# Keys and values in tiles of 96 local and 32 global rows, and one bank that takes values and global scores before either is read

## The chip, the cores and the metric

The kernel runs on one core of a Trainium2 chip. Its metric is the device time of one execution in microseconds (us), the median of several runs; the kernel before took 952.92 us (952.77 to 953.38 in 3 runs). A core has engines that run side by side, each with its own in-order queue: TensorE (PE, matrix products, with weight loads as PEld), VectorE (DVE), ScalarE (ACT), GpSimd (POOL) and SyncE (SP), which here issues nearly all transfers (DMAs). TensorE writes its products to PSUM, which has eight banks of 128 partitions x 512 floats; DVE and ACT read them from there.

## The reference

Three stages follow each other. Attention over 4 batches, 8 heads, 512 local tokens and 32 global ones, with a head size of 64:

```
k_all, v_all = concat(k_g, k_l), concat(v_g, v_l)          # 32 + 512 rows
out_g = softmax(q_g k_all^T / 8) v_all                     # global queries see everything
s_ll  = q_l k_l^T / 8, only where |i - j| <= 32            # local queries see a band ...
out_l = softmax(concat(q_l k_g^T / 8, s_ll)) v_all         # ... and the 32 global keys
```

Its 2176 rows of 512 go through two MLPs with weights 512 x 2048 and 2048 x 512: first `h = x @ w_in; max(0.01 h, h) @ w_out`, then `h = x @ w_in; (h - tanh(h)) @ w_out`. The MLP weights arrive as 64-bit floats and are converted in the kernel; each product runs as three products of high and low parts.

## The kernel before, in words

Attention is cut into 32 units, numbered `pp`: a batch, a half `a` of its 512 queries (256 of them), and two of the eight heads. Four heads of a half make a group `g` (two units), which is what is loaded at once. The 256 queries of a unit are eight blocks of 32 (index `i`). A block sees three blocks of local keys and the 32 global ones, so its scores are 32 x 128: a window of 128 columns in the transposed keys.

- `load_kq(g)` (L331) loads queries `qr` and keys `kr`; `kr` holds 320 key rows in three tiles of 112, 112 and 96. `load_v(g)` (L356) loads values into one of three `v_raw` tiles, 96 local rows and, in the last 32 partitions, the global ones.
- `k_prep(pp)` (L393) transposes the keys on PE, then ACT (L402) and DVE (L404, L405) copy them to `kt`, with the global 32 columns repeated after each 96 local ones. `q_prep` does the same for the queries.
- `score(pp)` writes the windows of both heads to two banks; `smax_a` takes the row minimum (DVE, in the later units together with the mask, L457) and the exponential (ACT, L464).
- `p_trans(pp)` (L468) transposes the exponentials, and ACT copies them to `pt`.
- `copy_v(pp)` (L371) has POOL copy the values to `vx`, shifted, so that each window has its 128 value rows in the order of its columns; L378 first repeats the global rows.
- `av(pp, ps)` (L489) multiplies `pt` by the values into the columns 0 to 259 of the bank `avps` (64 value columns and a sum for each of four head and half combinations). DVE then reads the bank: L500 and L501 make the reciprocal of the sum, L503 the division into `o`. `o_trans` (L506) transposes `o` into the bank `otps`, and ACT and DVE make the MLP's inputs `xh` and `xl` of it.
- `g_score(pp, ps)` (L548) multiplies the keys by the global queries; ACT copies the result to `sg`. From unit 10 on (`PRE`) it writes the columns from 260 on of the same bank that `av` has just used; before that it has a bank of its own (`sgps`).

`stage(s)` (L864) puts units behind one another: in stage s the keys of unit s+1 are prepared, unit s is scored, `cols` (L870) does `av` of unit s-2 and `g_score` of unit s, and `turns` does `p_trans` of unit s-1 and `o_trans` of unit s-2. In `cols` the order is: `av` with its reads by DVE, then `load_v`, `copy_v`, then `g_score` with its read by ACT.

Stages 0 to 9 come first, with little else on PE. Stages 10 to 33 lie between the steps of the first MLP (`mlp1_a` makes `h`, `mlp1_b` makes `y`): their operations are spread over its items, one after every few groups of three matmuls. From unit 10 on the stages use three banks in turn. Weights are converted beside them (`in_job`, `job`: L127, L131, L137, L142, then L149/L150 or L785/L788).

The order of PE is the written one as far as attention reaches (`fix`, L940, switches the planner off for PE). The other engines, SP's transfers among them, are ordered by a planner that simulates the program; each of them then works in that order and stands when its next instruction has to wait.

Of the kernel before, what the change touches and what calls it, by code (L numbers as in the profile page):

```python
# [8 lines left out]
F32 = mybir.dt.float32  # L9
# [12 lines left out]
def kernel(  # L22
# [265 lines left out]
    band = att.tile([BLK, 3 * BLK], mybir.dt.bfloat16, name="band", bufs=1)  # L288
# [5 lines left out]
    def build_masks():  # L294


# [3 lines left out]
        for at, step in ((0, 1), (2 * BLK, -1)):  # L300
# [6 lines left out]
        for i in range(8):  # L307
            j, u = divmod(i, 4)
            n = BLK * (3 - i % 3)
            for a in range(2):  # L310
                m = mask[BLK * u : BLK * u + BLK, a, j]
                nc.vector.tensor_copy(m[:, :n], band[:, :n])
                if n < 3 * BLK:
                    nc.vector.tensor_copy(m[:, n + BLK :], band[:, n:])
        nc.vector.memset(mask[:BLK, 0, 0, :BLK], BIG)
        nc.vector.memset(mask[3 * BLK :, 1, 1, 3 * BLK :], BIG)

    first_key = [0, SL - 288]
    KT = (0, 112, 224, 320)

# [3 lines left out]
    v_raw = [att.tile([128, 4, 4, D + 1], F32, name=f"vr{i}", bufs=1) for i in range(3)]  # L324
# [6 lines left out]
    def load_kq(g):  # L331
# [4 lines left out]
        qr = att.tile([128, 2, 4, D], F32, tag="qr", name="qr", bufs=2)  # L336
        kr = att.tile([128, 3, 4, D], F32, tag="kr", name="kr", bufs=2)

        for t in range(3):
            on = nc.scalar if g == 0 and t == 2 else nc.sync  # L340
            for r0, r1, loc in ((0, SG, a), (SG, 9 * BLK, 1), (9 * BLK, 10 * BLK, not a)):
                lo, hi = max(r0, KT[t]), min(r1, KT[t + 1])
                if lo >= hi:
                    continue
                k0 = a * HALF - BLK + lo
                src = k_l[b, hs, k0 : k0 + hi - lo, :] if loc else k_g[b, hs]
                on.dma_start(out=kr[lo - KT[t] : hi - KT[t], t], in_=src.rearrange("h s d -> s h d"))
        queue = nc.scalar if g < 2 else nc.sync
# [3 lines left out]
        for k in range(2):  # L352
            h2 = slice(2 * k, 2 * k + 2)
            raw_t[2 * g + k] = qr[:, :, h2, :], kr[:, :, h2, :]

    def load_v(g):  # L356
# [4 lines left out]
        for t, n in ((0, 96), (1, 96), (2, 96), (3, BLK)):  # L361
            k0 = a * HALF - BLK + 96 * t
            p0, p1 = max(0, -k0), min(n, SL - k0)
            if p0 < p1:
# [6 lines left out]
    def copy_v(pp):  # L371

        if pp >= NU // 2:
            return
# [774 lines left out]
```

## Time and profile before

| | |
|---|---|
| median of the runs | 952.92 us (952.77 to 953.38) |
| the profiled execution | 955.39 us |
| its span, from the first to the last instruction | 953.6 us |
| PE busy | 890.6 us, 93% |
| DVE, ACT, POOL busy | 619.0, 508.6, 129.3 us |
| mean granted clock of TensorE | 0.98 |

Each engine's busy time is the sum of its instructions; what is left to the span is idle time, and the trace names for each idle stretch the instruction that ended it. Stages 0 to 9 of the attention take the first 60 us or so, the stages among the first MLP's steps lie between about 60 and 160 us and between 250 and 440 us, and the second MLP runs from about 590 us on. The granted clock is given as a share of 2.4 GHz; 0.50 is its lower level of 1.2 GHz, and a value between says how much of the stretch each had.

### The profile page before, as it was taken

What the parts mean: (1) busy time and instruction counts of PE and PEld (TensorE: products, weight loads), DVE (VectorE), ACT (ScalarE), POOL (GpSimd) and SP (SyncE); (2) the same over time, 40 slices, a digit from 0 to 9 for tenths busy, and PEclk for the clock granted to TensorE, in tenths of its full rate; (3) what the DMA queues carried; (4) which work ended last, traced back from release to release, by engine and by line L of the source; (5) the groups of instructions that cost most, each with busy time, mean ns of one, the idle gap of its engine ahead of it and who ended that gap; (6) DMA issues with size and microseconds to landing.
All of it is one profiled execution on the core that took longest, in us unless ns stands there. A gap on an engine that the chain in (4) does not pass through costs nothing.

```text
span 953.6 us, 18518 instructions
## 1 busy us (share of the span) xinstructions
PE 890.6 (93%) x6940; PEld 752.2 (79%) x6940; DVE 619.0 (65%) x1395; ACT 508.6 (53%) x1093; POOL 129.3 (14%) x244
## 2 busy tenths in 40 slices
PE   6676888999989888989999999999999999999998
PEld 4455666888777787867888999888888888899997
DVE  5575556776554544553323347978888888888886
ACT  5665555544454455543333456656565655656565
POOL 4673321000122223220000000000000000000022
PEclk9897999999999999999999999999999999999999
DMA  7884667768876877665656575001100100010010
GB/s 170 200 181 109 183 191 239 247 181 270 250 224 202 243 214 219 211 200 185 192 174 214 192 254 174 9 1 34 45 0 1 67 1 1 1 45 0 1 35 23
DMA packets 129707, 128.35 MB, mean 135 GB/s; under 512 B 68177, under 2 KB 91985, under 8 KB 129617
## 3 DMA queue, kind: packets, MB, share of 16 engines
q1 hardware_dynamic: 126944, 126.42, 44.2%
q8 instruction: 54, 0.88, 0.4%
q10 hardware_dynamic: 2672, 0.75, 0.4%
q14 instruction: 37, 0.30, 0.1%
HBM read 100.40 MB, written 26.74 MB: 133 GB/s over the span
## 4 chain that ended last, share of the span: by engine, by line
PE 85%; DVE 7%; DMA 2%; ACT 2%; issue 1%; POOL 1%; SPq 1%; ACTq 0%; POOLq 0%; DVEq 0%
PE h L55 39%; PE y L55 20%; PE o L55 20%; DVE e L457 2%; DMA vr<-in_v_g_dram 1%; PE avps L55 1%; PE sps L55 1%; PE ptps L472 1%; PE gavps L55 1%; DVE o L503 1%; DVE wt L137 1%; PE kps L399 1%; PE otps L511 1%; DVE wf L142 1%; DMA inraw<-in_moe_w_in_dram 0%
## 5 line engine op out<-in xcount | busy, mean ns | idle before, releaser
L55 PE MATMUL h<-xh,win 128*128 128x512 f32 (+2 forms) x1280 | 357.4, 363 | 0.2 <-ACT g L213 0.2
L55 PEld LDWEIGHTS h<-xh,win 128*128 128x128 f32 x1280 | 232.7, 191 | 33.9 <-ACT g L213 0.8
L55 PE MATMUL h<-xl,win 128*128 128x512 f32 (+2 forms) x640 | 230.7, 360 | 0.0
L215 DVE TENSOR_TENSOR gl<-g,gh 128x512 fp32r<-128x512 f32 (+2 forms) x80 | 49.1, 613 | 134.4 <-ACT gh L214 121.6
L55 PEld LDWEIGHTS h<-xl,win 128*128 128x128 f32 x640 | 121.9, 190 | 15.6
L55 PE MATMUL y<-gh,woh 128*128 128x512 f32 (+2 forms) x320 | 120.3, 376 | 0.0
L55 PE MATMUL y<-gh,wol 128*128 128x512 f32 (+2 forms) x320 | 116.1, 363 | 0.0
L55 PE MATMUL y<-gl,woh 128*128 128x512 f32 (+2 forms) x320 | 115.9, 364 | 0.0
L213 ACT ACTIVATE g<-h 128x512 f32<-128x512 f32 (+2 forms) x80 | 42.7, 533 | 128.2 <-PE h L55 127.9
L55 PE MATMUL o<-wo2l,gh 128*128 128x512 f32 x255 | 99.6, 391 | 0.0
L55 PE MATMUL o<-wo2h,gh 128*128 128x512 f32 x255 | 99.4, 390 | 0.0
L55 PE MATMUL o<-wo2h,gl 128*128 128x512 f32 x255 | 97.4, 390 | 0.0
L675 ACT ACTIVATE u<-h 128x512 f32<-128x512 f32 (+2 forms) x80 | 42.6, 532 | 91.5 <-PE h L55 83.8
L701 POOL TENSOR_TENSOR gl<-p,gh 128x256 fp32r<-128x256 f32 x16 | 11.8, 739 | 509.0 <-ACT gh L700 504.7
L55 PEld LDWEIGHTS y<-gh,woh 128*128 128x128 f32 x320 | 61.2, 191 | 8.6 <-issue 1.3
L55 PEld LDWEIGHTS y<-gl,woh 128*128 128x128 f32 x320 | 61.4, 192 | 8.2
L700 ACT ACTIVATE gh<-p 128x512 fp32r<-128x512 f32 (+2 forms) x80 | 45.4, 568 | 40.9 <-DVE p L684 40.9
L55 PEld LDWEIGHTS y<-gh,wol 128*128 128x128 f32 x320 | 61.3, 192 | 6.8
L701 DVE TENSOR_TENSOR gl<-p,gh 128x512 fp32r<-128x512 f32 (+1 forms) x64 | 41.9, 654 | 21.9 <-ACT gh L700 21.8
L681 ACT ACTIVATE u<-u,consts 128x512 f32<-128x512 f32 (+2 forms) x80 | 52.7, 659 | 6.1 <-DVE p L679 3.4
L55 PEld LDWEIGHTS o<-wo2h,gl 128*128 128x128 f32 x255 | 47.9, 188 | 10.1
L55 PEld LDWEIGHTS o<-wo2l,gh 128*128 128x128 f32 x255 | 47.9, 188 | 9.0
(133 smaller groups left out, 1459.8 us busy)
## 6 DMA issues: line engine op xcount, KB each, us to landing
wraw<-in_moe_w_out_dram SPq DMA_DIRECT2D x32, 512.0 KB, 4.8
woh<-wod SPq DMA_DIRECT2D x64, 256.0 KB, 3.8
wol<-wod SPq DMA_DIRECT2D x64, 256.0 KB, 3.4
inraw<-in_moe_w_in_dram SPq DMA_DIRECT2D x16, 512.0 KB, 6.3
wraw<-in_moe_w_in_dram SPq DMA_DIRECT2D x16, 512.0 KB, 5.1
vn<-in_v_l_dram SPq DMA_DIRECT2D x8, 512.0 KB, 6.4
wod<-woh SPq DMA_DIRECT2D x16, 256.0 KB, 5.4
wod<-wol SPq DMA_DIRECT2D x16, 256.0 KB, 4.5
```

The costliest lines, as they stand in the source:

```text
L55: nc.tensor.matmul(o, lhsT, rhs, start=start, stop=stop, skip_group_check=shared)
L137: nc.vector.scalar_tensor_tensor(out=t[0], in0=hw, scalar=-0x80000000, in1=t[0], op0=ALU.bitwise_and, op1=ALU.bitwise_or)
L142: nc.vector.scalar_tensor_tensor(out=w.bitcast(I32), in0=lw, scalar=29, in1=t[0], op0=ALU.logical_shift_right, op1=ALU.bitwise_or)
L213: nc.scalar.activation(g[:, :N], h[:, :N], AF.Prelu, alpha=0.01)
L215: anchor[0] = nc.vector.tensor_sub(gl[:, :N], g[:, :N], f32(gh)[:, :N])
L399: nc.tensor.transpose(ps[:, KT[t] : KT[t + 1]], kr[:n, t].rearrange("p h d -> p (h d)"), ident[:n, :n])
L457: nc.vector.tensor_tensor_reduce(out=e[:, h, j], in0=ps[h][:, j * WIN : j * WIN + WIN], in1=mask[:, a, j], op0=ALU.add, op1=ALU.min, scale ...
L472: nc.tensor.transpose(ps[:, k * 128 : k * 128 + 128], e[:, k // 2, k % 2], ident)
L675: nc.scalar.activation(u, h, AF.Square)
L681: nc.scalar.activation(u, u, AF.Square, bias=tc_a2)
L700: nc.scalar.activation(gh[:, :N], p, AF.Copy)
L701: eng["pool" if i == order2[-1] else "dve"].tensor_sub(gl[:, :N], p, f32(gh)[:, :N])
```

## The change

- `cols` now lets `av` and `g_score` issue their matmuls one behind the other; each returns its reads (`av_out` on DVE, `g_out` on ACT), which are called after both. `load_v` and `copy_v` come after these.
- Keys are 288 local rows in three tiles of 96, with the 32 global rows as rows 96 to 127 of the first. One transpose has 128 rows, two have 96. DVE's second copy (L405) is gone. In the transposed keys the global columns stand before each 96 local ones in the first half (`a` = 0) and after them in the second.
- Values are three tiles of 96 local rows with the global rows before or after them. A window may now hold the global columns in any place (`window`, `block_at`); four of the eight windows of a unit use the loaded tile directly (three before), and `copy_v` makes four rotated tiles instead of five, with two copies of 64 partitions and four of 32.
- The masks are written block by block to fit these windows.
- `kr` and `qr` have three buffers instead of two, and `load_kq` is called one group further ahead: group 3 in stage 0, then group 2 behind that stage, then groups 4, 5, ... in stages 2, 4, ... A group takes 4 transfers of keys (5 before), 2 of queries and 4 of values (5 before, in the second half 4).

```diff
--- before.py
+++ after.py
@@ -285,43 +285,52 @@
     mask = att.tile([128, 2, 2, WIN], mybir.dt.bfloat16, name="mask", bufs=1)
-    band = att.tile([BLK, 3 * BLK], mybir.dt.bfloat16, name="band", bufs=1)
+    band = att.tile([BLK, 2 * BLK], mybir.dt.bfloat16, name="band", bufs=1)
     ident_b = att.tile([128, 128], mybir.dt.bfloat16, name="ident_b", bufs=1)
...
     def build_masks():
...
         make_identity(nc, ident)
...
         make_identity(nc, ident_b)
-        for at, step in ((0, 1), (2 * BLK, -1)):
+        for at, step in ((0, 1), (BLK, -1)):
             m = band[:, at : at + BLK]
...
         nc.vector.memset(mask, 0.0)
-        for i in range(8):
-            j, u = divmod(i, 4)
-            n = BLK * (3 - i % 3)
-            for a in range(2):
-                m = mask[BLK * u : BLK * u + BLK, a, j]
-                nc.vector.tensor_copy(m[:, :n], band[:, :n])
-                if n < 3 * BLK:
-                    nc.vector.tensor_copy(m[:, n + BLK :], band[:, n:])
-        nc.vector.memset(mask[:BLK, 0, 0, :BLK], BIG)
-        nc.vector.memset(mask[3 * BLK :, 1, 1, 3 * BLK :], BIG)
+        for a in range(2):
+            for i in range(8):
+                j, u = divmod(i, 4)
+                for k in range(4):
+                    m = mask[BLK * u : BLK * u + BLK, a, j, BLK * k : BLK * k + BLK]
+                    o = block_at(a, window(a, i) + k)
+                    if o is None:
+                        continue
+                    if not 0 <= o - i <= 2:
+                        nc.vector.memset(m, BIG)
+                    elif o - i != 1:
+                        nc.vector.tensor_copy(m, band[:, : BLK] if o == i else band[:, BLK:])
...
+    def block_at(a, x):
...
+        k, r = divmod(x, 4)
+        return (None if r == 3 else 3 * k + r) if a else (None if r == 0 else 3 * k + r)
...
+    def window(a, i):
...
+        if a:
+            return min(i + i // 3, 8)
+        return i + (i - 1) // 3 - ((i - 1) % 3 == 0) if i else 0
...
     first_key = [0, SL - 288]
-    KT = (0, 112, 224, 320)
...
     raw_t = {}
...
     v_t = {}
-    v_raw = [att.tile([128, 4, 4, D + 1], F32, name=f"vr{i}", bufs=1) for i in range(3)]
+    v_raw = [att.tile([128, 3, 4, D + 1], F32, name=f"vr{i}", bufs=1) for i in range(3)]
@@ -333,59 +342,59 @@
         b, a, hs = place_of(g)
-        qr = att.tile([128, 2, 4, D], F32, tag="qr", name="qr", bufs=2)
-        kr = att.tile([128, 3, 4, D], F32, tag="kr", name="kr", bufs=2)
...
+        qr = att.tile([128, 2, 4, D], F32, tag="qr", name="qr", bufs=3)
+        kr = att.tile([128, 3, 4, D], F32, tag="kr", name="kr", bufs=3)
...
+        k0 = first_key[a]
+        queue = nc.scalar if g < 2 else nc.sync
         for t in range(3):
             on = nc.scalar if g == 0 and t == 2 else nc.sync
-            for r0, r1, loc in ((0, SG, a), (SG, 9 * BLK, 1), (9 * BLK, 10 * BLK, not a)):
-                lo, hi = max(r0, KT[t]), min(r1, KT[t + 1])
-                if lo >= hi:
-                    continue
-                k0 = a * HALF - BLK + lo
-                src = k_l[b, hs, k0 : k0 + hi - lo, :] if loc else k_g[b, hs]
-                on.dma_start(out=kr[lo - KT[t] : hi - KT[t], t], in_=src.rearrange("h s d -> s h d"))
-        queue = nc.scalar if g < 2 else nc.sync
+            on.dma_start(out=kr[:96, t], in_=k_l[b, hs, k0 + 96 * t : k0 + 96 * t + 96, :].rearrange("h s d -> s h d"))
+            if t == 0:
+                nc.sync.dma_start(out=kr[96:, 0], in_=k_g[b, hs].rearrange("h s d -> s h d"))
         for t in range(2):
...
             h2 = slice(2 * k, 2 * k + 2)
-            raw_t[2 * g + k] = qr[:, :, h2, :], kr[:, :, h2, :]
+            raw_t[2 * g + k] = qr[:, :, h2], kr[:, :, h2]
...
         vr = v_raw[g % 3]
-        for t, n in ((0, 96), (1, 96), (2, 96), (3, BLK)):
-            k0 = a * HALF - BLK + 96 * t
-            p0, p1 = max(0, -k0), min(n, SL - k0)
-            if p0 < p1:
-                nc.sync.dma_start(
-                    out=vr[p0:p1, t, :, :D], in_=v_l[b, hs, k0 + p0 : k0 + p1, :].rearrange("h s d -> s h d")
-                )
-            if t == 0:
-                nc.sync.dma_start(out=vr[3 * BLK :, 0, :, :D], in_=v_g[b, hs].rearrange("h s d -> s h d"))
+        k0 = first_key[a]
+        loc, glob = (slice(0, 96), slice(96, 128)) if a else (slice(32, 128), slice(0, 32))
+        for t in range(3):
+            nc.sync.dma_start(
+                out=vr[loc, t, :, :D], in_=v_l[b, hs, k0 + 96 * t : k0 + 96 * t + 96, :].rearrange("h s d -> s h d")
+            )
+        nc.sync.dma_start(out=vr[glob, 0, :, :D], in_=v_g[b, hs].rearrange("h s d -> s h d"))
...
             return
+        a = pp // NP % 2
         v = v_raw[pp // 2 % 3].rearrange("p t h d -> p t (h d)")
...
         if pp % 2 == 0:
-            cp(v[96:, 1:3], v[96:, 0:1].to_broadcast([BLK, 2, 4 * (D + 1)]))
+            g = slice(96, 128) if a else slice(0, 32)
+            cp(v[g, 1:3], v[g, 0:1].to_broadcast([SG, 2, 4 * (D + 1)]))
         n = 2 * (D + 1)
         v = v[:, :, n * (pp % 2) : n * (pp % 2) + n]
-        x = att.tile([128, 5, n], F32, tag="vx", name="vx", bufs=2)
-        cp(x[:32, :3], v[32:64, :3])
-        cp(x[32:64, :3], v[64:96, :3])
-        cp(x[64:96, :3], v[96:, :3])
-        cp(x[96:, :3], v[:32, 1:])
-        cp(x[:64, 3:], v[64:, :2])
-        cp(x[64:, 3:], v[:64, 1:3])
-        v_t[pp] = [x[:, 3 * (i % 3 - 1) + i // 3] if i % 3 else v[:, i // 3] for i in range(8)]
+        x = att.tile([128, 4, n], F32, tag="vx", name="vx", bufs=2)
+        cp(x[:64, :2], v[64:, :2])
+        cp(x[64:, :2], v[:64, 1:])
+        sh = 1 if a else 3
+        for r in range(4):
+            w = (r + sh) % 4
+            cp(x[32 * r : 32 * r + 32, 2:], v[32 * w : 32 * w + 32, (r + sh) // 4 : (r + sh) // 4 + 2])
+        v_t[pp] = []
+        for i in range(8):
+            k, r = divmod(window(a, i), 4)
+            v_t[pp].append(v[:, k] if r == 0 else x[:, k if r == 2 else 2 + k])
@@ -395,23 +404,21 @@
         for t in range(3):
-            n = KT[t + 1] - KT[t]
-            nc.tensor.transpose(ps[:, KT[t] : KT[t + 1]], kr[:n, t].rearrange("p h d -> p (h d)"), ident[:n, :n])
-        kt = att.tile([128, 3 * WIN + BLK], F32, tag="kt", name="kt", bufs=2)
-        to = kt[:, : 3 * WIN].rearrange("p (k n) -> p k n", k=3)
-        nc.scalar.activation(to[:, :, : 3 * BLK], ps[:, : 9 * BLK].rearrange("p (k n) -> p k n", k=3), AF.Copy)
-        g0 = 9 * BLK * a
-        nc.vector.tensor_copy(to[:, :, 3 * BLK :], ps[:, g0 : g0 + SG].unsqueeze(1).to_broadcast([128, 3, SG]))
-        nc.vector.tensor_copy(kt[:, 3 * WIN :], ps[:, 9 * BLK : 10 * BLK])
+            n = 96 if t else 128
+            nc.tensor.transpose(ps[:, 128 * t : 128 * t + n], kr[:n, t].rearrange("p h d -> p (h d)"), ident[:n, :n])
+        kt = att.tile([128, 3 * WIN], F32, tag="kt", name="kt", bufs=2)
+        to = kt.rearrange("p (g n) -> p g n", g=3)
+        o = 0 if a else BLK
+        nc.scalar.activation(to[:, :, o : o + 96], ps[:, :384].rearrange("p (t n) -> p t n", t=3)[:, :, :96], AF.Copy)
+        o = 96 if a else 0
+        nc.vector.tensor_copy(to[:, :, o : o + SG], ps[:, 96:128].unsqueeze(1).to_broadcast([128, 3, SG]))
         k_t[pp] = kt
...
         for t in range(2):
-            nc.tensor.transpose(
-                ps[:, t * 128 : t * 128 + 128], qr[:, t].rearrange("p h d -> p (h d)"), ident
-            )
+            nc.tensor.transpose(ps[:, t * 128 : t * 128 + 128], qr[:, t].rearrange("p h d -> p (h d)"), ident)
         qt = att.tile([128, HALF], F32, tag="qt", name="qt", bufs=2)
@@ -432,7 +439,7 @@
             j, u = divmod(i, 4)
-            c = BLK * (i + i // 3)
+            c = BLK * window(a, i)
             for h in range(2):
@@ -495,6 +502,9 @@
                     mm(ps[BLK * u : BLK * u + BLK, c : c + D + 1], pt[:, h, BLK * i : BLK * i + BLK], v[i][:, (D + 1) * h : (D + 1) * h + D + 1], True, True)
+        return lambda: av_out(pp, ps)
...
+    def av_out(pp, ps):
         got = ps[:, : 4 * (D + 1)].rearrange("p (k n) -> p k n", k=4)
@@ -559,17 +569,18 @@
         kt = k_t[pp]
-        keys = [(0, kt[:, 0:96]), (96, kt[:, 128:160])]
-        keys.append((128, bass.AP(kt.tensor, kt.offset + 160, [kt.ap[0], (3 * BLK, 2), (1, 2 * BLK)])))
         if a:
-            keys.append((256, kt[:, 320:352]))
+            keys = [(0, kt[:, :96]), (96, kt[:, 128:160]), (128, kt[:, 160:224]), (192, kt[:, 256:352])]
+        else:
+            keys = [(0, kt[:, :128]), (128, kt[:, 160:256]), (224, kt[:, 288:320])]
         for c, x in reversed(keys):
...
                 o = ps[64 * i + SG * h : 64 * i + SG * h + SG, c - 128 * i : c - 128 * i + x.free_size()]
-                if len(x.shape) == 3:
-                    o = o.rearrange("p (k n) -> p k n", k=2)
                 mm(o, qg_t[b][:, p, SG * h : SG * h + SG], x, True, True)
+        return lambda: g_out(sg, r, n0, a, pp, ps)
...
+    def g_out(sg, r, n0, a, pp, ps):
         if pp < PRE:
@@ -869,14 +880,18 @@
             ps = bank(tag(), "avps")
+            outs = []
             if s >= 2:
-                av(s - 2, ps)
-                if s % 2:
-                    load_v((s + 3) // 2)
+                outs.append(av(s - 2, ps))
+            if s <= last:
+                outs.append(g_score(s, ps[:, 4 * (D + 1) :] if s >= PRE else bank(tag(), "sgps")))
+            for o in outs:
+                o()
+            if s >= 2 and s % 2:
+                load_v((s + 3) // 2)
             if s >= 1:
...
             if s <= last:
-                g_score(s, ps[:, 4 * (D + 1) :] if s >= PRE else bank(tag(), "sgps"))
                 hv, p = divmod(s, NP)
@@ -901,7 +916,7 @@
             if s % 2 == 0:
-                load_kq((s + 4) // 2)
+                load_kq((s + 6) // 2)
@@ -974,7 +989,6 @@
         for t in v_raw:
-            nc.gpsimd.memset(t[:BLK, 0:4:3], 0.0)
             nc.gpsimd.memset(t[:, :, :, D], 1.0)
@@ -1002,6 +1016,8 @@
                 in_load()
+            if pp == 0:
+                load_kq(2)
             if pp < 2:
```

## Rows read from the trace of the kernel before

**Rows 1.** The page: span, busy time by engine, PE in 40 slices (tenths).

```profile
span 953.6 us, 18518 instructions
...
PE 890.6 (93%) x6940; PEld 752.2 (79%) x6940; DVE 619.0 (65%) x1395; ACT 508.6 (53%) x1093; POOL 129.3 (14%) x244
...
PE   6676888999989888989999999999999999999998
```

**Rows 2.** Windows: PE, PEld, DVE, ACT, POOL busy; clock, DMA share, GB/s.

```profile
60.00:80.00 20.00, 13.69 (x204) 10.29 (x202) 12.08 (x43) 12.21 (x32) 9.87 (x17) 0.83 0.60 131
...
160.00:180.00 20.00, 20.00 (x105) 16.35 (x105) 14.55 (x27) 10.46 (x20) 0.00 (x0) 1.00 0.79 258
...
240.00:260.00 20.00, 18.77 (x155) 15.04 (x154) 11.81 (x29) 9.57 (x20) 2.78 (x6) 1.00 0.91 259
```

**Rows 3.** Waits of PE, whole span: who, for whom; us, times, longest.

```profile
PE avps L55 <- DVE o L503: 36.3, 22, 4.7
PE otps L511 <- DVE o L503: 7.6, 6, 1.7
PE avps L55 <- POOL vx L385: 4.4, 1, 4.4
```

**Rows 4.** Waits of PE, 80 to 165 us.

```profile
PE avps L55 <- DVE o L503: 15.9, 7, 4.7
```

**Rows 5.** Waits of PE, 165 to 440 us.

```profile
PE avps L55 <- DVE o L503: 19.1, 14, 2.1
```

**Rows 6.** Timeline of PE: start, us, instruction; in brackets the idle time before.

```profile
80.17 0.44 PE L55 MATMUL avps<-kt,qgd 128*32 128x128 f32 x12 [2.93 <-DVE o L503]
...
89.23 0.22 PE L55 MATMUL avps<-vx,pt 128*32 128x65 f32 x1
94.13 0.75 PE L55 MATMUL avps<-kt,qgd 128*32 128x32 f32 x16 [4.69 <-DVE o L503]
...
99.42 0.38 PE L511 MATMUL otps<-ident,o 128*128 128x128 f32 x2
...
105.51 0.48 PE L55 MATMUL avps<-kt,qgd 128*32 128x32 f32 x16 [1.23 <-DVE o L503]
...
107.84 0.38 PE L511 MATMUL otps<-ident,o 128*128 128x128 f32 x2
...
340.25 0.44 PE L55 MATMUL avps<-kt,qgd 128*32 128x128 f32 x12 [1.42 <-DVE o L503]
```

**Rows 7.** Timeline of DVE at 93 and 104 us.

```profile
93.66 0.41 DVE L503 TENSOR_TENSOR o<-avps,sum 128x256 f32<-128x256 f32 x1
...
104.63 0.16 DVE L500 TENSOR_SCALAR sum<-avps 128x4 f32<-128x4 f32 x1
...
105.03 0.42 DVE L503 TENSOR_TENSOR o<-avps,sum 128x256 f32<-128x256 f32 x1
```

**Rows 8.** Windows of 4 us with a lower granted clock; columns as above.

```profile
44.00:48.00 4.00, 4.00 (x42) 3.19 (x49) 0.91 (x4) 2.61 (x7) 3.26 (x7) 0.50 0.56 122
...
80.00:84.00 4.00, 3.83 (x42) 3.11 (x43) 1.09 (x3) 0.97 (x4) 2.26 (x4) 0.77 0.72 222
...
92.00:96.00 4.00, 1.87 (x36) 1.47 (x36) 2.77 (x6) 1.20 (x3) 1.89 (x3) 0.55 0.73 165
...
340.00:344.00 4.00, 3.75 (x45) 3.56 (x46) 0.39 (x2) 0.87 (x4) 1.81 (x4) 0.70 0.82 174
...
428.00:432.00 4.00, 4.00 (x15) 3.21 (x14) 1.33 (x4) 0.79 (x2) 0.00 (x0) 0.71 0.44 136
```

**Rows 9.** Timeline of POOL in the first stages.

```profile
37.91 0.62 POOL L378 COPY vr<-vr 32x520 f32<-32x520 f32 x1 [6.82 <-DMA vr<-in_v_g_dram]
```

**Rows 10.** Timeline of SP's queue, 10 to 17 us.

```profile
10.94 2.12 SPq L347 DMA_DIRECT2D kr<-in_k_l_dram  x4
...
14.87 1.36 SPq L365 DMA_DIRECT2D vr<-in_v_l_dram  x1
```

**Rows 11.** Groups of instructions by line and form: count, busy us, mean ns.

```profile
L578 ACT ACTIVATE sg<-avps 64x128 f32<-64x128 f32 x32 | 8.6, 270 | 8.8 <-PE avps L55 7.6
```

## The prediction, made before the result was known

> **What bounds the kernel now.** I read the page's first two parts, then the windows, then the waits of TensorE (PE below), then the timelines around the longest waits. PE is busy 890.6 of 953.6 us, so 63.0 us are idle [rows 1]. The windows say where: at 160 to 180 us, where only the MLP runs, PE is busy 20.00 of 20 us; from 60 to 80 us, with attention stages beside the MLP, 13.69; from 240 to 260 us 18.77 [rows 2]. From about 450 us on, slice 20 of the page's 40, PE is at nine tenths or more in nearly every slice [rows 1], and the change touches nothing there. So the idle time lies in the attention stages, in two stretches: the first 60 us with ten stages that have little beside them, and the 22 stages (10 to 31) that run between MLP steps.
>
> In the 22 stages one wait makes nearly all of it: the first global score matmul waits for DVE's division L503 of the values, 36.3 us in 22 waits, at most 4.7; of the rest only 4.4 us behind POOL's copies and 7.6 us of output transposes (otps) behind L503 are large [rows 3]. Of the 36.3, seven waits with 15.9 us lie in 80 to 165 us and 14 with 19.1 us in 165 to 440 us [rows 4, 5]; the one left, 1.4, lies at 69 us. Both sets of matmuls write one PSUM bank, and PE takes its instructions in the written order: it finishes the value matmuls, stands until DVE has read them, and then writes the scores. At 104 us the shortest form is seen: DVE starts L500 at 104.63 and ends L503 at 105.45, and PE goes on at 105.51 after 1.23 us [rows 6, 7]. At 89 us it is the longest: the last value matmul starts at 89.23, DVE does weight conversions first, L503 starts at 93.66 and ends at 94.07, and PE resumes at 94.13 after 4.69 us [rows 6, 7].
>
> **The change, part by part.** The sum is made against the profiled execution, 955.39 us, which stands 2.47 us above the median of 952.92; its span is 953.6 and 1.8 us lie around it.
>
> 1. *Values and scores are both written, then both read.* The wait inside the bank goes: minus 36.3 us, 22 times [rows 3]. Nothing else is taken off PE; the six or eight score matmuls per stage have the same columns as before. What is late next is otps, which needs L503's result. L503 now starts after the scores too (0.48 us for 16 of them at 105.51 [rows 6]), so its result comes at least 1.23 + 0.48 = 1.7 us after the last value matmul. In the written order otps stands behind the scores, MLP matmuls and four transposes: 107.84 - 105.51 = 2.33 us after the scores begin [rows 6], one of the shortest such distances. So where the wait is 1.2 to 1.8 us nothing returns. At 89 us DVE is loaded with its own work until 93.66 and otps would stand ready at 89.44 + (99.42 - 94.13) = 94.7 at the slow clock of that moment, some 3 us after 89.44 at the fast one: about 1.7 us come back. The next longest, 2.93 us before 80.17 [rows 6], is shorter than those 3 us. Plus 1.7.
>
> 2. *Other waits grow, since PE no longer lets DVE and ACT catch up.* The covers are PE's own waits; the resource is DVE and ACT at 12.08 and 12.21 of 20 us while PE ran at 13.69 [rows 2]. Bounds: nothing, and the whole 15.9 + 1.4 = 17.3 us of the first eight stages. DVE has 40% idle there even now, so I take it near the low end: plus 3.
>
> 3. *The clock.* After the 4.69 us wait the granted clock is 0.55 in 92 to 96 us, that is mostly the 1.2 GHz level. There are eleven windows of 4 us like this directly behind waits for L503, from 80 us (0.77) to 428 us (0.71), the others 0.80, 0.55, 0.60, 0.60, 0.80, 0.77, 0.70, 0.88, 0.86 [rows 8]. One minus each, times 4 us, sums to 11.8 us of lost full-speed time; about 2 of it fell on idle time. Bounds: 0, if other idle spots keep the clock down, and 10. I take 8, because item 1 leaves only one such wait: minus 8. The row of 340 to 344 us shows a fall to 0.70 right behind a wait of only 1.42 us [rows 8, 6]. A rule of the Trainium skill speaks against counting that one ("TensorE: Matmul & The Clock Gate", section "HAM oscillation — how this bites in real kernels"): it blames long idle gaps only. By it only the 4.69 us wait would have cost clock, 1.8 + 1.6 us, and this term would be minus 3.4 and the time 919.4; the row disagrees, and the measurement decides.
>
> 4. *The loads.* Keys and queries go to three buffers and one group further ahead, with 6 DMAs for 7, values 4 for 5. Bytes are the same. SP issues almost without pause in the first 30 us: group 2's loads take it from 10.94 to 14.7 and the values of group 1 go out at 14.87 [rows 10]. Now group 3's loads are issued in stage 0 before group 2's and before those values: 6 issues at about 0.55 us, 3.3 us later, less 1 us from the shorter v0 and kq lists. POOL is queued in order behind these: its L378 stood 6.82 us, to 37.9 us, for one group's global values, the copies for PE stood behind it, and PE waited 4.4 us for them [rows 9, 3]. A delay of up to 3 us may pass into the first stages, twice at most: plus 6. If the jam at 37 us dissolves, those 4.4 us go and the slow clock behind it (0.50 in 44 to 48 us, 2 us, and part of the four before [rows 8]; 3 us in all): minus 7.4. Near the middle, nearest to the delayed values: plus 1.5. The other new wait: the buffers rotate 0, 1, 3, 2, so group 5's load must wait for group 3's transposes in stage 6. Behind it on SP stand values of group 4 and weights; they are wanted from stage 9, some 10 us later, so it costs nothing unless POOL again takes them too early.
>
> 5. *The small edits.* DVE's copy L405 goes, 32 times, in DVE's free time: 0 to minus 1. POOL copies per pair: four of 390 columns become four of 260, two of 64 partitions stay; POOL is busy 14% of the span [rows 1], and its copies count only where PE waited those 4.4 us: 0 to minus 1. Masks are written by 32 small DVE instructions instead of 28, at the start, within 0.5. Transposes of 128, 96, 96 instead of 112, 112, 96 rows: nothing. Together 0.
>
> Sum: -36.3 + 1.7 + 3 - 8 + 1.5 = -38.1. 955.4 - 38.1 = 917.3 for a profiled execution; less 2.5, the median is about 915 us.
>
> **The rivals.** *A. Half of it is eaten.* The first eight interleaved stages turn bound by the chains DVE to ACT to PE, and the clock stays low there: items 2 and 3 come out at +12 and -3, the front at +4. -36.3 + 1.7 + 12 - 3 + 4 = -21.6: about 931. For it: DVE and ACT are 60% busy there and in order. Against: the 14 later waits, 19.1 us, lie where PE is otherwise full [rows 5, 2].
> *B. The readers take turns, ACT first.* L503 would then stand behind ACT's two copies of the scores (2 x 0.27 us [rows 11]) and behind whatever ACT does before them, up to some 1.5 us; then otps waits about 1 us in most stages, 22 us come back, and the gain is 36.3 - 22 + 3 of clock = 17: about 936. Against: the value read is written first in the program. The Trainium skill ("PSUM — Partial Sum Buffer", section "PSUM bank collisions raise a hardware error") says that no two engines may touch one bank's quadrant at once, two readers included; no row here shows two readers at once in this bank, and by the rule some order there must be.
> *C. Slower: the loads jam.* Place: SP's queue with group 3 before group 2 and group 5 held till stage 6; POOL's L378 in front of copies that PE wants. Price: each jam is 4.4 us of wait plus 3 us of slow clock, 7.4 us, as now at 37 to 48 us [rows 3, 8, 9]. It decides from the sixth jam on (36.3 + 8 - 4.7 - 1.5 = 38.1 is the gain it must undo): 6 x 7.4 - 38.1 = +6, about 959. For it: one such jam is there now. Against: only some six groups go through in the stages with little MLP work, and they are issued with fewer DMAs.
> *D. It doesn't do what it says*: the score matmuls still wait, or otps takes over the whole wait: 950 to 953. Against: PE's order is the written order.
> *E. Better*: the jam at 37 us goes too and no wait grows: -36.3 - 10 - 7.4 = -53.7: about 899.
>
> **The numbers.** Forecast 0.65, A 0.13, B 0.05, C 0.04, D 0.03, E 0.10. The forecast with its own bounds goes from 903 to 925; with most of E below and of A above the range is 900 to 932, leaving out a fifth. 0.2% of this time, 1.9 us, is about what a measurement can tell from no change. Faster 0.94, same 0.02, slower 0.04.
>
> **What would show it.** In the profile after: no wait of avps matmuls for DVE L503; otps waits for it of under 3 us in all in the 22 stages (over 15: B or D); PE's idle from 160 to 440 us near zero, so that stretch is 19 to 22 us shorter; the granted clock 1.00 in the later stages; if the first 60 us grew by more than 6 us, the loads are the cause. The forecast is wrong if PE's idle in the interleaved stages stays above 15 us.

## The result and the profile after

The changed kernel takes 906.98 us in the median of 4 runs (906.01 to 909.04), beside 953.12 (952.77 to 953.38) for the kernel before. The ratio is 0.9519, with an interval of 0.9501 to 0.9537: 46.1 us less, where 38.1 had been forecast. The profiled execution took 909.04 us with a span of 906.9.

The page of the kernel after, beside [rows 1]: PE is 876.7 us busy, so 30.2 of the span are idle, 32.8 less than before. The busy time fell too, by 13.9 us, with the same 6940 matmuls. From the fifth slice on all are nines but the last.

```profile
span 906.9 us, 18456 instructions
...
PE 876.7 (97%) x6940; PEld 743.0 (82%) x6940; DVE 613.3 (68%) x1367; ACT 506.2 (56%) x1093; POOL 110.0 (12%) x241
...
PE   6678999999999999999999999999999999999998
```

The waits of PE after, over the whole span (us, times, longest), against [rows 3]: the 36.3 us of avps behind DVE's division (it was L503 and is L513 now) are gone as a row. What heads the list is the wait of the output transposes (otps), as large as before.

```profile
PE otps L521 <- DVE o L513: 7.7, 7, 2.5
PE kps L408 <- DMA kr<-in_k_g_dram: 4.3, 1, 4.3
PE avps L55 <- ACT pt L481: 2.5, 2, 1.6
...
PE avps L55 <- POOL vx L389: 0.5, 1, 0.5
```

To see where the time went, both spans are cut at the same points of the work (the output transposes of units 7, 15, 16 and 30). The windows of the kernel before (length, busy time of PE, PEld, DVE, ACT and POOL, granted clock, DMA share, GB/s):

```profile
0.00:62.30 62.30, 42.42 (x891) 31.57 (x891) 37.93 (x128) 38.49 (x108) 38.19 (x83) 0.95 0.76 186
62.30:153.88 91.58, 72.38 (x948) 55.37 (x948) 52.50 (x173) 51.06 (x130) 31.78 (x57) 0.87 0.65 179
153.88:261.76 107.88, 106.65 (x579) 87.14 (x578) 72.82 (x132) 52.74 (x95) 3.20 (x7) 1.00 0.75 230
261.76:448.08 186.32, 167.89 (x2020) 143.67 (x2018) 91.51 (x303) 91.22 (x234) 44.27 (x83) 0.98 0.70 212
448.08:953.60 505.52, 501.30 (x2512) 434.48 (x2510) 364.26 (x659) 275.11 (x528) 11.82 (x16) 1.00 0.22 71
```

and the same windows of the kernel after:

```profile
0.00:62.09 62.09, 44.25 (x890) 32.57 (x891) 36.50 (x121) 38.57 (x108) 32.53 (x81) 0.89 0.88 200
62.09:129.78 67.69, 62.40 (x948) 48.01 (x948) 50.68 (x165) 50.04 (x130) 26.42 (x55) 1.00 0.76 217
129.78:238.00 108.22, 106.56 (x579) 87.05 (x578) 72.65 (x131) 52.71 (x95) 3.00 (x7) 1.00 0.80 240
238.00:401.36 163.36, 162.18 (x2020) 140.93 (x2018) 89.48 (x291) 90.01 (x234) 36.21 (x83) 1.00 0.79 240
401.36:906.90 505.54, 501.33 (x2512) 434.42 (x2510) 364.01 (x659) 274.85 (x528) 11.81 (x16) 1.00 0.21 71
```

The gain lies in two of the five stretches: 23.9 us in the second and 23.0 in the fourth. In each it has two parts, read from length and PE busy. Idle time fell from 19.2 to 5.3 us in the second (minus 13.9) and from 18.4 to 1.2 in the fourth (minus 17.2). Busy time fell by 10.0 and 5.7 us for the same instructions. Most of that is the clock, whose column goes from 0.87 to 1.00 and from 0.98 to 1.00; the rest is taken apart in the section on the prediction. The front stretch is as long as it was in this execution (idle 2.0 us less, busy 1.8 more at 0.89 for 0.95), and the MLP's tail has not moved.

### The profile page after: what moved, and what is told of

Same layout as the page of the kernel before. It is cut to its first block, busy times and chain, and to the rows that moved or that the text cites. A ratio compares the mean times of both kernels' runs of the same rounds, so it can differ in the third digit from the quotient of the medians.

```text
span 906.9 us, 18456 instructions
## 1 busy us (share of the span) xinstructions
PE 876.7 (97%) x6940; PEld 743.0 (82%) x6940; DVE 613.3 (68%) x1367; ACT 506.2 (56%) x1093; POOL 110.0 (12%) x241
## 4 chain that ended last, share of the span: by engine, by line
PE 90%; DVE 4%; ACT 3%; DMA 2%; issue 1%; SPq 0%; ACTq 0%
PE h L55 40%; PE o L55 21%; PE y L55 20%; PE sps L55 2%; PE avps L55 2%; PE gavps L55 1%; PE kps L408 1%; PE ptps L479 1%; DMA inraw<-in_moe_w_in_dram 1%; PE otps L521 1%; PE qps L421 1%; DMA vg<-in_v_g_dram 1%; DVE wt L137 1%; DVE wf L142 0%; DMA kr<-in_k_l_dram 0%
## 5 line engine op out<-in xcount | busy, mean ns | idle before, releaser
L55 PE MATMUL h<-xh,win 128*128 128x512 f32 (+2 forms) x1280 | 353.4, 360 | 0.6 <-ACT g L213 0.6
L55 PEld LDWEIGHTS h<-xh,win 128*128 128x128 f32 x1280 | 230.1, 188 | 34.1 <-ACT g L213 1.7
L55 PE MATMUL y<-gl,woh 128*128 128x512 f32 (+2 forms) x320 | 113.9, 357 | 0.0
L712 POOL TENSOR_TENSOR gl<-p,gh 128x256 fp32r<-128x256 f32 x16 | 11.8, 738 | 506.3 <-ACT gh L711 502.3
L393 POOL COPY vx<-vr 32x260 f32<-32x260 f32 x128 | 57.3, 448 | 6.5
```

Source lines behind the costliest of these rows:

```text
L55: nc.tensor.matmul(o, lhsT, rhs, start=start, stop=stop, skip_group_check=shared)
L393: cp(x[32 * r : 32 * r + 32, 2:], v[32 * w : 32 * w + 32, (r + sh) // 4 : (r + sh) // 4 + 2])
L712: eng["pool" if i == order2[-1] else "dve"].tensor_sub(gl[:, :N], p, f32(gh)[:, :N])
```

## The experiments

Each ran beside the kernel before. The ratio is that of the mean times, with its 95% interval; "idle" is, in its profile, the span less PE's busy time.

| kernel | median us | before, beside it | ratio, interval | PE idle | PE busy |
|---|---|---|---|---|---|
| order only | 913.5 | 952.19 | 0.9588 (0.9562 to 0.9614) | 35.6 | 876.5 |
| layout only | 949.1 | 952.19 | 0.9958 (0.9940 to 0.9976) | 58.4 | 884.8 |
| ten products in the wait | 960.65 | 952.19 | 1.0080 (1.0049 to 1.0111) | 31.5 | 927.5 |
| loads near | 908.74 | 952.19 | 0.9535 (0.9505 to 0.9564) | 30.1 | 873.8 |
| changed kernel again | 906.63 | 955.23 | 0.9496 (0.9465 to 0.9527) | 29.9 | 874.7 |
| five products in the wait | 945.96 | 955.23 | 0.9906 (0.9876 to 0.9936) | 36.3 | 908.7 |
| group 2 before 3 | 907.77 | 955.23 | 0.9510 (0.9483 to 0.9537) | 30.0 | 875.0 |
| otps later in the front | 905.19 | 955.23 | 0.9485 (0.9453 to 0.9517) | 28.5 | 873.7 |
| order early only | 931.76 | 953.1 | 0.9773 (0.9748 to 0.9798) | 48.2 | 880.5 |
| order late only | 925.03 | 953.1 | 0.9696 (0.9671 to 0.9721) | 42.8 | 881.8 |
| no cover | 945.67 | 953.1 | 0.9915 (0.9893 to 0.9938) | 60.0 | 884.7 |

**The order alone.** The kernel before, with only the order of the bank's writers and readers changed:

```diff
+            outs = []
             if s >= 2:
-                av(s - 2, ps)
-                if s % 2:
-                    load_v((s + 3) // 2)
+                outs.append(av(s - 2, ps))
+            if s <= last:
+                outs.append(g_score(s, ps[:, 4 * (D + 1) :] if s >= PRE else bank(tag(), "sgps")))
+            for o in outs:
+                o()
+            if s >= 2 and s % 2:
+                load_v((s + 3) // 2)
             if s >= 1:
                 copy_v(s - 1)
             if s <= last:
-                g_score(s, ps[:, 4 * (D + 1) :] if s >= PRE else bank(tag(), "sgps"))
```

> The kernel before with the order of the change alone: values and scores both written, then both read; layout, loads and copies as before. Theory (the order is all): 907, within 4, the waits of avps for L503 gone, PE idle from 62 to 154 us down by about 14 us, and TensorE's busy time down by 10 to 16 us since the slow clock goes too. Rival (layout and loads carry a part, in the first 60 us or by lighter POOL and DVE work): 915 to 930.

It gains 38.7 us, some 6.5 short of the changed kernel's time, which I had expected of it: 913.5 lies between the two ranges, and beside the order the layout is worth something after all. PE's busy time is that of the changed kernel (876.5 beside 876.7), so its whole fall is the order's. The stretch that was 91.58 us long is 69.10 at a clock of 1.00 (windows of this kernel, columns as above):

```profile
63.72:132.82 69.10, 62.26 (x947) 47.77 (x948) 51.76 (x173) 50.18 (x130) 32.02 (x56) 1.00 0.72 208
```

What it lacks of the changed kernel, 5.2 us of span, is idle time, and its waits of PE show one that the changed kernel has only in small (0.5 us at most, 1.8 in its second profile): the first stages still wait for POOL's copies of the values, as in [rows 3].

```profile
PE avps L55 <- POOL vx L385: 4.9, 1, 4.9
```

**The layout alone.** The changed kernel with the old order:

```diff
-            outs = []
             if s >= 2:
-                outs.append(av(s - 2, ps))
-            if s <= last:
-                outs.append(g_score(s, ps[:, 4 * (D + 1) :] if s >= PRE else bank(tag(), "sgps")))
-            for o in outs:
-                o()
-            if s >= 2 and s % 2:
-                load_v((s + 3) // 2)
+                av(s - 2, ps)()
+                if s % 2:
+                    load_v((s + 3) // 2)
             if s >= 1:
                 copy_v(s - 1)
             if s <= last:
+                g_score(s, ps[:, 4 * (D + 1) :] if s >= PRE else bank(tag(), "sgps"))()
```

> The changed kernel with the old order in its stages: the values are read by DVE before the scores are written; the new layout, loads, copies and masks stay. Theory (the order is all): 953, within 4, with some 36 us of waits for DVE's division back. Rival (layout and loads carry a part): under 945.

The wait is back nearly in full (35.3 of 36.3 us), and the layout is worth 0.2 to 0.6%, some 2 to 6 us. The profiled execution, whose idle and busy time stand in the table, was the fastest of nine, 4 us below the median:

```profile
PE avps L55 <- DVE o L513: 35.3, 22, 3.8
```

**The waiting filled with products of zeros.** If a PE that waits costs clock beyond the wait itself, a PE that is kept busy while it waits should run its other work faster, though its place in the order is unchanged. Kernel before, ten products of 128x128 zeros in 20 of the 22 stages, added to y or to a free bank:

```diff
+            if PRE <= s <= PRE + 2 or PRE <= s <= last and y_open[0]:
+                fill = y_ps[0] if y_open[0] else bank("y3", "fill")
+                for _ in range(10):
+                    mm(fill[:, :128], zero, ident, not y_open[0], False, True)
             if s <= last:
                 g_score(s, ps[:, 4 * (D + 1) :] if s >= PRE else bank(tag(), "sgps"))
```

> The kernel before, with ten extra 128x128 products of zeros (about 1.1 us at the fast clock) on PE between values and scores in 20 of the 22 interleaved stages, into another bank. They add zeros only. PE waits no longer idle but just as long. Theory (some 14 us of the gain are the clock, which falls because PE stands idle there): the waits shrink to under 15 us, the stages stay as far apart, but the granted clock stays near 1.00 from 62 us on and the time falls to 938 to 945. Rival (all the gain is the wait itself, and the lower clock has other causes): 953 to 957.

The size was wrong: one product of fp32 stands in the trace as two matmuls, so ten took 2.50 us, longer than most of the waits. The timeline of PE in one stage (the next scores follow without a wait):

```profile
98.10 2.50 PE L55 MATMUL y<-ident,zero 128*128 128x128 f32 x20
100.53 0.48 PE L55 MATMUL avps<-kt,qgd 128*32 128x32 f32 x16
```

So the kernel got slower, and both ranges were missed. It can still be read: its two groups of zero products are 42.5 + 7.5 = 50.0 us of the busy time, and the rest, 927.5 - 50.0 = 877.5, is 13.1 less than the 890.6 of [rows 1]. The same edit with five products:

```diff
-                for _ in range(10):
+                for _ in range(5):
```

> As the kernel that filled the wait, with five products of zeros for ten: each shows as two matmul records of about 0.125 us, so ten were 2.5 us, twice the shortest wait, and five are 1.25 us. Theory (the lower clock comes from PE standing idle there, and costs some 14 us): waits for L503 under 15 us, the interleaved stages at a granted clock of 0.97 or more, and 938 to 946. Rival (the lower clock has other causes): 950 to 956.

This one gains 9.3 us, though in every stage the scores still have to come after DVE's reads. Its groups of instructions (count, busy us, mean ns, idle before) put the products at 23.5 + 4.1 = 27.6 us:

```profile
L55 PE MATMUL y<-ident,zero 128*128 128x128 f32 x170 | 23.5, 285 | 0.0
L55 PE MATMUL fill<-ident,zero 128*128 128x128 f32 x30 | 4.1, 285 | 0.0
```

Idle time fell by 63.0 - 36.3 = 26.7, so filling and idling cancel; the other work fell to 908.7 - 27.6 = 881.1, 9.5 us less. Most of that is clock: the same stretch runs at 0.98 instead of 0.87, and the one low window of 4 us left in it stands behind a gap of 2.77 us that the five products didn't fill (windows of this kernel):

```profile
63.48:146.53 83.05, 74.28 (x1028) 58.49 (x1029) 52.54 (x173) 50.51 (x130) 32.09 (x56) 0.98 0.67 190
...
92.00:96.00 4.00, 4.00 (x29) 3.26 (x25) 0.79 (x2) 1.56 (x5) 0.07 (x1) 0.57 0.78 229
```

Two single stages show it more sharply. A stage is cut here from one unit's output transposes to the next's. First stage 26, whose clock was 1.00 all along, then stage 24, where it had been 0.87. The kernel before:

```profile
354.73:365.27 10.54, 9.31 (x142) 8.67 (x141) 4.88 (x20) 6.08 (x17) 3.44 (x7) 1.00 0.93 249
332.40:345.52 13.12, 11.70 (x163) 10.84 (x162) 5.69 (x22) 6.18 (x18) 3.44 (x7) 0.87 0.78 215
```

The kernel with five products:

```profile
346.29:356.83 10.54, 10.54 (x152) 9.85 (x151) 4.89 (x20) 6.09 (x17) 3.45 (x7) 1.00 0.92 252
325.48:337.09 11.61, 11.50 (x172) 10.52 (x171) 5.71 (x22) 6.18 (x18) 3.59 (x7) 1.00 0.79 195
```

Stage 26 kept its length to the last digit: the products fill the wait and do nothing else. Its busy time rose by 1.23 us, though the products took 1.38: they overlap with the matmuls beside them, and some 0.15 us for each of the 20 stages, 3 of the 9.5 us, is not clock. Stage 24 got 1.51 us shorter, at a clock of 1.00. In the seven stages whose clock had been below 1.00 the other work fell by 11.5 us with five products and by 11.8 with ten, about 1 us of it this overlap. Over whole executions the granted clock was 0.989 to 0.995 in the four runs with five products and 0.978 to 0.984 in the seven of the kernel before beside them.

**Early or late stages.** The changed kernel with the new order only below stage 18, and only from it on:

```diff
-                outs.append(av(s - 2, ps))
+                o = av(s - 2, ps)
+                outs.append(o) if s < 18 else o()
```

> The changed kernel with the new order in stages 0 to 17 alone; from stage 18 on the values are read before the scores are written, as before. Theory (each wait is worth itself plus its clock, and the two stretches add up): the stretch from 130 us to the end loses the 19.1 us of waits and about 4 of clock, 928 to 932. Rival (the gain sits in the crowded first stretch and the later waits are hidden otherwise): under 918.

```diff
-                outs.append(av(s - 2, ps))
+                o = av(s - 2, ps)
+                outs.append(o) if s >= 18 else o()
```

> The mirror of it: the new order from stage 18 on, the old one before. Theory: the first interleaved stretch loses its 24 us (17.3 of waits and 10 of clock, less what had come back), 927 to 933; the two losses together are the whole difference between the old and the new order. Rival (under 918 or over 940): the stretches are not independent.

The waits left over are 19.1 us in 14 stages and 16.3 in 8 (waits of PE of the first and then of the second):

```profile
PE avps L55 <- DVE o L513: 19.1, 14, 2.1
```

```profile
PE avps L55 <- DVE o L513: 16.3, 8, 3.8
```

The first came out as expected; the second, 925.03, 2 us below its range. Against the 906.63 of the changed kernel, the first loses 25.1 us and the second 18.4. Together 43.5, beside 949.1 - 906.6 = 42.5 where all stages lose it: to within some 3 us, by which the runs of one kernel differ, the stages add up.

**Without the cover.** The forecast rests on the PE work that stands between the scores and the output transposes. Here the transposes, in the stages from 10 on, follow right behind the two readers:

```diff
             for o in outs:
                 o()
+            if s >= PRE:
+                o_trans(s - 2, tag())
...
-            if s >= 2:
+            if 2 <= s < PRE:
                 o_trans(s - 2, tag())
```

> The changed kernel with the transposes otps of the interleaved stages right behind the scores, where before some MLP products and four transposes stand between. Theory (the division by DVE is hidden only because other work of PE stands ahead of its next use): otps waits for L503's result 1.2 to 1.7 us in each of the 22 stages, 27 to 37 us in all, and with the clock the time is 935 to 950, as good as the whole gain gone. Rival (DVE is done sooner, since no wait holds its queue up): waits under 15 us, and under 925.

Nearly the whole wait moves over: 34.4 of the 41.8 us below lie behind 60 us, for the 36.3 that went. Much of PE's busy time comes back with it, 8.0 of the 13.9 us. 7.4 us remain (0.6 to 1.1%), a little more than the layout's 2 to 6 alone. Its waits of PE:

```profile
PE otps L521 <- DVE o L513: 41.8, 30, 3.6
```

and its window of the second stretch, which is cut a little earlier in the order here (918 matmuls for 948):

```profile
59.89:145.07 85.18, 66.57 (x918) 50.80 (x918) 50.85 (x164) 50.21 (x127) 27.73 (x57) 0.90 0.70 193
```

**The loads.** The changed kernel with two buffers and loads no further ahead than before, then with the loads of group 2 ahead of those of group 3:

```diff
-        qr = att.tile([128, 2, 4, D], F32, tag="qr", name="qr", bufs=3)
-        kr = att.tile([128, 3, 4, D], F32, tag="kr", name="kr", bufs=3)
+        qr = att.tile([128, 2, 4, D], F32, tag="qr", name="qr", bufs=2)
+        kr = att.tile([128, 3, 4, D], F32, tag="kr", name="kr", bufs=2)
...
-                load_kq((s + 6) // 2)
+                load_kq((s + 4) // 2)
...
-            if pp == 0:
-                load_kq(2)
```

> The changed kernel with the loads of keys and queries as before: two buffers, one group less ahead, groups in order. Theory (the loads are neutral, as the first 62 us are equal in both kernels): 907, within 3. Rival (the early loads help the interleaved stages): 912 or more. Rival (issuing group 3 before group 2 costs in the first stages): 903 or less.

```diff
             if s % 2 == 0:
+                load_kq(2) if s == 0 else None
                 load_kq((s + 6) // 2)
...
-            if pp == 0:
-                load_kq(2)
```

> The changed kernel with group 2's keys and queries issued before group 3's, both in stage 0; nothing else. Theory (the swapped order costs nothing): 907, within 3, the same as the changed kernel beside it. Rival (it delays the first stages and holds group 5's load): 903 or less.

Neither can be told from the changed kernel, which ran again beside the second (the intervals of the ratios overlap, and the medians lie within 2.1 us of each other):

> The changed kernel once more, beside the next three on one chip. Both theories: 907, within 3.

So neither the distance of the loads nor their order is worth more than some 3 us here, in either direction.

**Output transposes later in the front.** The changed kernel's largest wait left is otps in the first ten stages. There the transposes were put one stage's preparation later:

```diff
             q_prep(s + 1, tag())
+            if 3 <= s <= PRE:
+                o_trans(s - 3, tag())
...
-            if s >= 2:
+            if s >= 2 and s >= PRE:
                 o_trans(s - 2, tag())
```

> The changed kernel with the same idea carried to the first ten stages: the transposes otps, which wait there for L503, are issued one operation later, behind the next stage's transposes of keys and queries. Theory (a wait of PE goes where other work of PE is put ahead of it): the waits of otps for L503 in the first 62 us fall from 7.7 to under 2, and the time by 3 to 7, to 900 to 904. Rival (DVE and ACT bound these stages, and the wait comes back before the scores or the next values): 906 to 909.

Both ranges of the expectation were missed. The wait shrank from 6.3 us in the changed kernel's second profile to 4.2, and others came up behind it (waits of PE of this kernel):

```profile
PE otps L521 <- DVE o L513: 4.2, 3, 2.4
...
PE kps L408 <- DVE xl L645: 1.8, 1, 1.8
```

The intervals of the two overlap, so whether it beats the changed kernel is open.

## Why the prediction was right, and where its sizes were off

**The wait goes (step 1): right.** 36.3 us were to go and 36.3 went; with the old order on the new layout 35.3 are there. In the 22 stages 1.7 us were to come back at otps. The waits of PE after, from 62 to 402 us, show 1.6, and most of it stands for ACT:

```profile
PE otps L521 <- ACT sg L589: 1.4, 2, 1.1
...
PE otps L521 <- DVE o L513: 0.2, 1, 0.2
```

The run without the cover shows that this holds only because of the matmuls in between. What step 1 missed is that each removed wait brought some 0.2 us more than its length (see the clock below).

**Other waits (step 2): right.** Steps 1 and 2 were to bring 4.7 us back; in the three middle stretches, idle outside the removed wait was 38.9 - 36.3 = 2.6 us before and is 8.1 after, so some 5.5 came back.

**The clock (step 3): mis-sized, and a term beside it was missing.** Minus 8 was forecast, with a bound of minus 10. PE's busy time in the three middle stretches fell by 15.8 us (10.0, 0.1 and 5.7); the 1.8 that this execution lost again in the front are counted under step 4. So 7.8 of the 8.6 us by which the span's gain (46.7) exceeds the forecast lie here; the rest is step 4, 1.7 better than forecast, less some 0.9 of steps 1 and 2.

But not all of the 15.8 us is clock. Of the 22 stages 15 ran at 1.00 before and after, and in them too PE's busy time fell, by 3.0 us in all. Stage 26, before in the lines of the five products, and here in the kernel after, is 1.43 us shorter, though only 1.23 us of waiting went (stage 24 beside it):

```profile
319.67:328.78 9.11, 9.11 (x142) 8.60 (x141) 5.18 (x19) 5.73 (x17) 2.42 (x6) 1.00 1.00 294
301.28:311.89 10.61, 10.03 (x162) 9.29 (x161) 5.68 (x22) 6.84 (x20) 3.40 (x7) 1.00 0.91 243
```

The timeline of PE shows where the other 0.20 us was. Before, the last value matmul runs to its end, then PE waits, then the scores start:

```profile
361.49 0.22 PE L55 MATMUL avps<-vx,pt 128*32 128x65 f32 x1
362.93 0.44 PE L55 MATMUL avps<-kt,qgd 128*32 128x128 f32 x12 [1.23 <-DVE o L503]
```

After, the scores start 0.05 us behind the last value matmul, while it still runs:

```profile
326.41 0.22 PE L55 MATMUL avps<-vr,pt 128*32 128x65 f32 x1
326.46 0.43 PE L55 MATMUL avps<-kt,qgd 128*32 128x32 f32 x12
```

The two runs with one order early and the other late agree: the same stage has 9.29 us of busy time where the old order is left in it and 9.10 where the new one is, both at 1.00. So a wait of PE costs its length and some 0.2 us of lost overlap, 4.4 us for 22 waits. The step that failed here is "Nothing else is taken off PE": this term stood at nothing.

The other 11.4 us are clock, in the seven stages that ran below 1.00 before (stage 24: 0.87); 0.2 us of overlap is taken off each of them too, an estimate from the other 15. The count behind the 8 was good: eleven windows with 11.8 us, less 2 on idle time, leave 9.8, and the six stages in which they lie lost 10.3. What failed is "I take 8", which took off 2 more, and "There are eleven windows of 4 us like this", counted from 80 us on. The seventh stage, with 1.1 us, lies before that; its windows in the kernel before are as low, behind the one wait for L503 that the prediction puts at 69 us:

```profile
68.00:72.00 4.00, 2.60 (x18) 1.93 (x19) 1.27 (x9) 1.82 (x6) 2.81 (x6) 0.56 0.45 83
72.00:76.00 4.00, 4.00 (x20) 3.07 (x19) 0.78 (x3) 2.63 (x7) 0.00 (x0) 0.58 0.00 0
```

Near 0.5 means that most of the stretch went at 1.2 GHz. Before the fall PE had stood 1.20 us for the keys at 66.72, and then 1.4 us for L503. In the changed kernel the wait for the keys is still there, with 1.43 us, and the second is gone; the clock stays (timeline of PE, then windows, of the kernel after):

```profile
66.76 0.66 PE L55 MATMUL sps<-kt,qt 64*32 64x128 f32 x30 [1.43 <-DVE kt L414]
```

```profile
68.00:72.00 4.00, 3.57 (x34) 2.54 (x23) 1.98 (x13) 3.57 (x11) 2.38 (x6) 1.00 0.19 44
72.00:76.00 4.00, 3.72 (x103) 2.77 (x102) 3.47 (x14) 2.84 (x8) 1.83 (x4) 1.00 0.23 53
```

The clock's column alone would have come near: one minus the clock, times PE's busy time, is (1 - 0.87) x 72.38 + (1 - 0.98) x 167.89 = 12.8 us, and the column's two digits leave some 1.2 us open. Taken with the length of the stretches it gives 15.6, but that this meets the 15.8 is chance, since those hold 4.4 us that aren't clock.

That the wait causes the loss, and not the other way round, is shown by the zero products: they kept the wait's place, and in the seven stages gave about as much back, 10.5 and 10.8 us with their overlap taken off. Why only seven of 22 waits cost clock stays open: the 1.42 us at 340.25 were followed by 0.70 [rows 6, 8], an equal wait at 329.29 by no lower window.

The Trainium skill has a section that fits better than the one weighed in the prediction: "TensorE: Matmul & The Clock Gate", section "A second HAM failure mode: psum-queue depth-cycling", tells of a kernel whose PE pauses briefly and often between groups of matmuls, so that the clock goes up and down. This trace agrees for seven of its 22 waits of 1.2 to 4.7 us, in which no load is involved: 0.70 behind one of 1.42 [rows 8, 6], but 1.00 in the 15 other stages.

**The loads (step 4): sign missed, small.** Plus 1.5 against minus 0.2 in the front of the profile, and minus 2 to 6 for the whole layout alone. The second profile of the changed kernel has its front 3.1 us shorter than the kernel before (its end and PE's busy time, columns as above):

```profile
0.00:59.23 59.23, 42.18 (x891) 31.39 (x891) 35.63 (x121) 38.35 (x108) 32.22 (x81) 0.94 0.92 210
```

The jam at 37 us was to dissolve only at the lower bound, minus 7.4, and it did, in both profiles: POOL makes these copies before it turns to the next group's global values (timeline of POOL after, against [rows 9]), and PE doesn't wait for them. Other waits for POOL's copies are left, 0.7 us here and 3.6 in the second profile, for 6.0 before.

```profile
32.47 1.71 POOL L393 COPY vx<-vr 32x260 f32<-32x260 f32 x4
...
39.52 0.62 POOL L384 COPY vr<-vr 32x520 f32<-32x520 f32 x1 [5.34 <-PE avps L55]
```

In the first profile the 5.3 us were eaten in the same stretch: 2.5 by waits for ACT's `pt`, where there had been none, 1.3 by otps and 1.8 by busy time at the lower clock. Distance and order of the loads, on which the plus rested, cost nothing that the runs could tell. Which part of the layout brings its few us (the tiles of the values with POOL's copies, those of the keys, or the fewer transfers) was not tried apart.

**The rivals.** A (half eaten), C (jam) and D (no change) did not come; the run without the cover shows what D's second form, otps with the whole wait, would have cost. E's time, 899, was not reached, but its minus 10 for the clock was nearer than the forecast. B's order came out the other way: DVE first, then ACT, which starts when DVE is done (timeline at 235 us after):

```profile
235.26 0.42 DVE L513 TENSOR_TENSOR o<-avps,sum 128x256 f32<-128x256 f32 x1
...
235.78 0.56 ACT L589 ACTIVATE sg<-avps 64x128 f32<-64x128 f32 x2 [0.16 <-DVE o L513]
```

The two readers of the bank do take turns, as the Trainium skill's "PSUM — Partial Sum Buffer" (section "PSUM bank collisions raise a hardware error") asks for; the price was at most the 1.4 us of otps behind ACT.

## What to carry to other kernels

Where two products share a bank and have different readers, write both and then read both, if PE has other work before the results are wanted: the wait inside the bank then costs nothing, and without that work it only changes its name. Size the clock's part of a gain by stretch, as one minus the granted clock, times PE's busy time (12.8 us for 11.4 here), and look at every low window, not only at those behind the longest waits. A wait that recurs among PE's matmuls can cost more than its length: here 36.3 us of waiting took with them some 11 us of clock and 4.4 us of overlap between matmuls.

## What was not expected of the chip

One wait of 1.43 us left the clock at 1.00, while 1.20 and 1.4 us shortly after one another were followed by 0.56 and 0.58. Products of zeros in the waiting time hold the clock nearly as well as the removal of the wait does: in the seven stages they gave back 10.5 us with five and 10.8 with ten, for 11.4. Even at a clock of 1.00 each wait took some 0.2 us of PE beside its length. A product of 128x128 in fp32 shows as two matmuls in the trace, ten of them in 2.50 us and five in 1.38.
